# Strided and local attention followed by a spectral mix: PE's order written out with one mode between pieces, local heads with full rows, the last product made by groups of modes

## The chip, the cores and the metric

The kernel runs on one core of a Trainium2 chip. The metric is the time of one execution on the device, in microseconds, median of the runs. The engines are PE (matmul), DVE, ACT, POOL and SP; POOL and SP also issue the DMAs here. Inputs and output lie in HBM as float32; the kernel computes in float16 with float32 accumulation.

## What is computed

```python
# attention: q, k, v are (8, 8, 576, 64)
mask_local = (rel >= 0) & (rel < 32)                      # heads 0 to 3
mask_strided = (rel >= 0) & (pos_k % 32 == pos_q % 32)    # heads 4 to 7
attn = softmax(where(mask, q @ k.T / 8, -1e9)); x = attn @ v   # (8, 576, 512)
# spectral mix, w_r and w_i are (64, 512, 512)
X = rfft(x, axis=1)[:, :64]
Yr = einsum(Xr, w_r) - einsum(Xi, w_i); Yi = einsum(Xr, w_i) + einsum(Xi, w_r)
u = x + irfft(Yr + 1j * Yi, n=576)
out = u + relu(u @ w_ch)
```

`rel` is the query's position less the key's; the einsums multiply each of 64 modes with its own 512x512 matrix.

## The kernel before

The work goes in four stages.

**Strided heads** (loop L622 to L638). For each of 8 batches `load_str` (L176) fetches q, k, v; `str_front` turns q and k on PE into `qT` and `kz`; `str_scores` multiplies six blocks, with the mask added by a matmul with the identity, and ACT takes the exponential into one of two buffers `P`; `str_values` multiplies with v; `normalise` writes `xb`. `dft` (L428) is the forward Fourier transform as a matmul. `w_fetch` (L155) meanwhile fills 12 weight buffers of 512 KB each (`pw`). All of w_r and w_i goes through them as 128 tiles: the 64 modes for input channels 256 to 511 first (slot 0), then for 0 to 255 (slot 1). POOL issues these DMAs, the q and k loads and part of v, in order in its queue; SP issues the rest of v and the output.

**Local heads with slot 0** (L651 to L656). For each batch the code is written as `attn_loc`, `dft`, and `modes(b, 0)` with eight modes. In `attn_loc` two heads share the array as 64-row halves (`pr`), keys of the 32 positions before a block are multiplied as 32-row tiles (L376, L409). A mode is 16 matmuls of 128x128 weights with 16 columns (L471), after which its buffer is free for the next `w_fetch`. Eight modes fill one PSUM tile `y`; ACT copies it to `Y0`.

**Prepare with slot 1** (L661 to L663). `prepare` turns `xb` into `xT`, and computes for 5 row tiles x @ w_ch into `v0` and x itself into `xo`. `modes(b, 1)` then adds its `y` to `Y0` and gives `YT` (L485).

**Finish** (L664). For each batch the transpose `yy` of YT (L562) and its product with w_ch, `zz` (L571), then for each row tile two accumulations in PSUM: v0 plus the inverse transform `cA` of zz (L586, L589), and xo plus that of yy (L593, L596). ACT takes relu of the first into `rl` (L600), DVE adds the second (L601), and SP sends it out.

The order on each engine is not that of the code: a scheduler places each instruction by a cost of its own among those that are ready, within the waits for data and buffers.

Of the kernel before, what the change touches and what calls it, by code (L numbers as in the profile page):

```python
# [15 lines left out]
B = 8  # L16
# [10 lines left out]
NWBUF = 12  # L27


def _host_consts():  # L30
# [16 lines left out]
    A = np.zeros((2 * NM, S))  # L47
    for mm in range(NM):
        e = np.zeros(S // 2 + 1, dtype=np.complex128)
        e[mm] = 1.0  # L50
        A[mm] = np.fft.irfft(e, n=S)
        e[mm] = 1j
        A[NM + mm] = np.fft.irfft(e, n=S)

# [12 lines left out]
    k = np.arange(128)[:, None]  # L67
    q = np.arange(128)[None, :]
    own = np.where((q - k >= 0) & (q - k < STRIDE), 0.0, NEG)
    mo = np.tile(own, (1, 4))  # L70
    mm_ = np.zeros((128, 384))
    mm_[:64, :128] = np.tile(own[:64, :64], (1, 2))
    kk = np.arange(32)[:, None]
    qq = np.arange(32)[None, :]
    mm_[96:, 128:] = np.tile(np.where(qq < kk, 0.0, NEG), (1, 8))
    f16 = [a.astype(np.float16) for a in (Fl, Fs, A, ms[0], ms[1], mo, mm_)]
# [4 lines left out]
def kernel(  # L81
# [15 lines left out]
    ps_tp = ctx.enter_context(tc.tile_pool(name="ps_tp", bufs=2, space=PSUM))  # L97
    ps_sc = ctx.enter_context(tc.tile_pool(name="ps_sc", bufs=2, space=PSUM))
    ps_av = ctx.enter_context(tc.tile_pool(name="ps_av", bufs=2, space=PSUM))
    ps_y = ctx.enter_context(tc.tile_pool(name="ps_y", bufs=2, space=PSUM))  # L100

    def psum_tp():
        return ps_tp.tile([128, 1024], F16, tag="tp", name="tp")

    def psum_sc():
        return ps_sc.tile([128, 512], FP, tag="sc", name="sc")

    def psum_av():
        return ps_av.tile([128, 512], FP, tag="av", name="av")

    def psum_y():
        return ps_y.tile([128, 512], FP, tag="y", name="y")

    hosts = _host_consts()
    names = ["cFl", "cFs", "cA", "cM6", "cM5", "cMo", "cMm", "cI"]
# [7 lines left out]
    w_cp = consts.tile([128, 4, DM], F16, name="w_cp")  # L123
# [8 lines left out]
    Y0 = big.tile([128, NM, 4, 16], F16, name="Y0")  # L132
    YT = big.tile([128, 4, B, 2, NM], F16, name="YT")
    xb = [px.tile([128, 11, 256], F16, tag="xb", name="xb") for _ in range(B)]

    wctx = ctx.enter_context(ExitStack())
    pw = wctx.enter_context(tc.tile_pool(name="pw", bufs=NWBUF))
# [6 lines left out]
    Ps = [pat.tile([128, 2816], F16, name=f"P{i}") for i in range(2)]  # L144
    v16 = [pat.tile([128, 12, 132], F16, name=f"v16_{i}") for i in range(3)]

    def clear(i):
        nc.vector.memset(kzs[i], 0.0)
        nc.vector.memset(Ps[i], 1.0)
# [3 lines left out]
    w_tiles, w_chs = [], []  # L153

    def w_fetch(n=1):  # L155
        for _ in range(n):
            i = len(w_tiles)
            if i == 2 * NM and not w_chs:
                w_ch = pw.tile([128, 4, DM], F16, tag="w", name="w_ch")
                nc.gpsimd.dma_start(  # L160
                    w_ch, moe_w_ch.rearrange("(c p) e -> p c e", p=128)
                )
                w_chs.append(w_ch)
            if i >= 2 * NM:
                return
            half, m = 1 - i // NM, i % NM
            wt = pw.tile([128, 4, DM], F16, tag="w", name="wt")
            for ri, src in enumerate([moe_w_r, moe_w_i]):
                nc.gpsimd.dma_start(  # L169
                    wt[ds(64 * ri, 64)],  # L170
                    src[m, ds(256 * half, 256), :].rearrange("(p c) e -> p c e", c=4),
                )
            w_tiles.append(wt)


    def load_str(b, early=None):  # L176
        qn = pin.tile([128, 2, 2048], F16, tag="qn", name="qn")
        for i, src in enumerate([q, k]):
            nc.gpsimd.dma_start(
                qn[0:72, i, :],  # L180
                src[b, 4:8].rearrange("h (c r) d -> (h c) (r d)", r=32),
            )
        vg = v16[b % 3]
        v32 = pin.tile([128, 8, 128], FP, tag="v32", bufs=2, name="v32")
        for j, (a, z) in enumerate(JG):
            n = (z - a) * NCB
            for h in range(4):
                src = v[b, 4 + h].rearrange("(c r2 rp) d -> c r2 (rp d)", r2=16, rp=2)
                if j == 0:
                    nc.gpsimd.dma_start(vg[0:n, h, 2:130], src[:, a:z, :])  # L190
                else:
                    nc.sync.dma_start(v32[0:n, 4 * j - 4 + h, :], src[:, a:z, :])
        return qn, v32

    def load_loc(b):
        qn = pin.tile([128, 2, 2048], F16, tag="qn", name="qn")
        for i, src in enumerate([q, k]):
            nc.gpsimd.dma_start(
                qn[:, i, 0:1152],
                src[b, 0:4].rearrange("h (cb i) d -> (h cb) (i d)", i=18),  # L200
            )
        v32 = pin.tile([128, 20, 64], FP, tag="v32", bufs=2, name="v32")
        for t in range(5):
            nc.sync.dma_start(
                v32[0 : SCS[t], ds(4 * t, 4), :],
                v[b, 0:4, ds(128 * t, SCS[t]), :].rearrange("h s d -> s h d"),
            )
        return qn, v32
# [19 lines left out]
    def str_front(b, qn, v32, part):  # L228
        qT, kz, vg = qTs[b % 2], kzs[b % 2], v16[b % 3]
        if part == 0:  # L230
            nc.gpsimd.tensor_copy(out=vg[0:90, 4:12, 2:130], in_=v32[0:90])
        tp = psum_tp()
# [40 lines left out]
    def str_scores(b, t):  # L273
        qT, kz, P = qTs[b % 2], kzs[b % 2], Ps[b % 2]
# [4 lines left out]
        scp = psum_sc()  # L279
        nc.tensor.matmul(scp[:, 0 : 4 * n], idn, mask, start=True, stop=False)  # L280
        for h in range(4):
# [8 lines left out]
            out=P[0:n, ds(POFF[t], 4 * n)],  # L290
# [5 lines left out]
    def str_values(b, t):  # L296
        P, vg = Ps[b % 2], v16[b % 3]
        j, rp = STR[t]
        n = (JG[j][1] - JG[j][0]) * NCB
        avp = psum_av()  # L300
        av = avp[:, 0:264].rearrange("p (h c) -> p h c", c=66)
        for h in range(4):
            nc.tensor.matmul(
                av[:, h, 0:65],
                P[0:n, ds(POFF[t] + n * h, 128)],
# [13 lines left out]
    def attn_loc(b, qn, v32):  # L319
        qT, P, vg = kzs[b % 2], Ps[b % 2], v16[b % 3]  # L320
        nc.gpsimd.tensor_copy(  # L321
            out=vg[:, 0:8, 2:130],
            in_=v32[:, 0:16, :].rearrange("p (g i) d -> p g (i d)", i=2),
        )
        nc.gpsimd.tensor_copy(
            out=vg[0:64, 8:10, 2:130],
            in_=v32[0:64, 16:20, :].rearrange("p (g i) d -> p g (i d)", i=2),
        )
        for vi in range(2):
            for g in range(2):  # L330
                tp = psum_tp()
                for i in range(9):
                    for hp in range(2):
                        nc.tensor.transpose(  # L334
                            tp[ds(64 * hp, 64), ds(64 * i, 64)],
                            qn[ds(64 * hp, 64), vi, ds(64 * (9 * g + i), 64)],
                            idn[ds(64 * hp, 64), ds(64 * hp, 64)],
                        )
                nc.vector.tensor_copy(  # L339
                    out=qT[:, vi, 0:1152].rearrange("p (h s i) -> p h s i", h=2, i=18)[  # L340
                        :, :, :, ds(9 * g, 9)
                    ],
                    in_=tp[:, 0:576].rearrange("p (i h s) -> p h s i", h=2, s=32),
                )
        for hp in range(2):
            pr = ds(64 * hp, 64)
            for hh in range(2):
                scp = psum_sc()
                nc.tensor.matmul(scp, idn, cs["cMo"], start=True, stop=False)  # L349
                for t in range(4):  # L350
                    nc.tensor.matmul(  # L351
                        scp[:, ds(128 * t, 128)],
                        qT[pr, 1, ds(576 * hh + 128 * t, 128)],
                        qT[pr, 0, ds(576 * hh + 128 * t, 128)],
                        start=False,
                        stop=(t == 3),
                    )
                nc.scalar.activation(  # L358
                    out=P[:, ds(512 * (2 * hp + hh), 512)],
                    in_=scp,  # L360
                    func=ACTF.Exp,
                    scale=SCALE,
                )
            scp = psum_sc()
            nc.tensor.matmul(scp[:, 0:384], idn, cs["cMm"], start=True, stop=True)
            for hh in range(2):
                nc.tensor.matmul(
                    scp[0:64, ds(64 * hh, 64)],
                    qT[pr, 1, ds(576 * hh + 512, 64)],
                    qT[pr, 0, ds(576 * hh + 512, 64)],  # L370
                    start=False,
                    stop=True,
                    skip_group_check=True,
                )
                for t in range(1, 5):
                    nc.tensor.matmul(  # L376
                        scp[96:128, ds(128 + 128 * hh + 32 * (t - 1), 32)],
                        qT[pr, 1, ds(576 * hh + 128 * t - 32, 32)],
# [317 lines left out]
```

## Time and profile before

| | |
|---|---|
| median of 3 runs | 519.66 us (518.39 to 520.14) |
| profiled execution | 520.25 us, span 518.5 us |
| busy: PE, PEld, DVE, ACT, POOL | 388.7, 252.5, 205.7, 134.7, 190.5 us |
| chain that ended last: PE, DMA, DVE | 49%, 38%, 5% |
| DMA moved | 97.50 MB at 188 GB/s; HBM read 165.78 MB, written 9.44 MB |

Busy time is an average over stages with different limits, so the rows to read are those by stage, and within a stage what was waited for last. PE's busy time is not PE at its peak. A wait of an engine matters only where the engine is on the chain.

### The profile page before, as it was taken

To read this page: it belongs to the slowest core of one execution; us is meant where nothing else is said; L and a number is where in the kernel's file an instruction comes from. 1 tells how busy PE (TensorE), PEld (TensorE's weight loads), DVE (VectorE), ACT (ScalarE), POOL (GpSimd) and SP (SyncE) were. 2 spreads that over 40 slices of the span, in tenths; PEclk is the share of its full clock that TensorE was granted. 3 is DMA by queue.
4 is the path that set the end of the run, shared out by engine and by line. 5 is a ranking of instruction groups with operands and counts; after the bars stand their busy time and mean duration, and the time that the engine had idled before them with its cause. 6 is when DMAs were issued, how large, how long until landed. Compare 5 with 4: busy or idle time off the path is not lost.

```text
span 518.5 us, 11415 instructions
## 1 busy us (share of the span) xinstructions
PE 388.7 (75%) x4832; PEld 252.5 (49%) x4832; DVE 205.7 (40%) x426; ACT 134.7 (26%) x257; POOL 190.5 (37%) x353
## 2 busy tenths in 40 slices
PE   3867787699999972569989998798972222239996
PEld 2655555556666652247646655465562222224332
DVE  6545445632414302024113556766450110125564
ACT  2545446222122120101321222232210000005553
POOL 5655654325343143515344434432253444300000
PEclk9978657755556555555555689998785555559999
DMA  8999989999999759999998999999799999965454
GB/s 165 184 193 181 188 156 186 197 183 196 211 212 211 143 88 207 212 209 169 213 211 157 211 212 212 212 213 190 126 168 212 212 211 212 211 114 183 183 184 182
DMA packets 61634, 97.50 MB, mean 188 GB/s; under 512 B 31760, under 2 KB 39312, under 8 KB 61584
## 3 DMA queue, kind: packets, MB, share of 16 engines
q0 software_dynamic: 32080, 78.51, 80.3%
q1 hardware_dynamic: 28928, 17.73, 12.8%
q8 instruction: 38, 0.62, 0.4%
q10 hardware_dynamic: 576, 0.53, 0.3%
q14 instruction: 12, 0.10, 0.0%
HBM read 165.78 MB, written 9.44 MB: 338 GB/s over the span
## 4 chain that ended last, share of the span: by engine, by line
PE 49%; DMA 38%; DVE 5%; issue 2%; ACT 2%; POOL 2%; SPq 1%; POOLq 0%; ACTq 0%; DVEq 0%
DMA wt<-in_moe_w_i_dram 25%; PE y L471 6%; DMA qn<-in_k_dram 5%; PE y L439 4%; PE sc L538 4%; PE av L401 4%; DMA qn<-in_q_dram 4%; PE av L409 3%; PE tp L334 3%; PE sc L351 3%; PE sc L349 2%; PE sc L586 2%; DMA wt<-in_moe_w_r_dram 2%; PE av L596 2%; PE av L593 2%
## 5 line engine op out<-in xcount | busy, mean ns | idle before, releaser
L169 POOL DMA_DIRECT2D wt<-in_moe_w_r_dram x128 | 67.1, 524 | 149.4 <-PE y L471 64.6
L471 PE MATMUL y<-X,wt 128*128 128x16 f16 x2048 | 72.4, 192 | 56.8 <-DMA wt<-in_moe_w_i_dram 56.1
L471 PEld LDWEIGHTS <-wt 128*128 128x128 f16 x2048 | 67.1, 105 | 66.8 <-issue 64.9
L169 POOL DMA_DIRECT2D wt<-in_moe_w_i_dram x128 | 67.6, 528 | 54.6 <-DMA wt<-in_moe_w_i_dram 45.2
L538 PE MATMUL sc<-w_cp,xT 128*128 128x512 f16 (+1 forms) x160 | 55.3, 420 | 2.6 <-DVE xT L526 2.0
L216 DVE RECIPROCAL rec<-av 90x4 f32<-90x4 f32 (+2 forms) x80 | 14.5, 182 | 102.4 <-PE av L409 79.1
L485 DVE TENSOR_TENSOR YT<-y,Y 128x512 f16<-128x512 f32 x8 | 19.5, 2437 | 70.3 <-PE y L471 70.3
L546 ACT ACTIVATE v<-sc 128x512 f16<-128x512 f32 (+1 forms) x40 | 23.8, 595 | 65.9 <-PE sc L538 65.9
L547 DVE COPY xo<-tp 128x512 f16<-128x512 f16 (+1 forms) x40 | 27.7, 695 | 31.7 <-PE tp L545 31.6
L339 DVE COPY kz<-tp 128x576 f16<-128x576 f16 x32 | 23.8, 756 | 34.4 <-PE tp L334 33.9
L401 PE MATMUL av<-v,P 128*128 128x65 f16 (+1 forms) x160 | 32.1, 236 | 6.9 <-POOL v L321 5.3
L545 PE MATMUL tp<-cI_s,xT 128*128 128x128 f16 (+1 forms) x160 | 35.6, 234 | 1.5 <-DVE xo L547 1.5
L334 PE MATMUL tp<-cI_s,qn 64*64 64x64 f16 x576 | 23.4, 239 | 17.6 <-DMA qn<-in_q_dram 16.4
L217 DVE TENSOR_TENSOR xb<-av,rec 90x256 f16<-90x256 f32 (+2 forms) x80 | 34.9, 443 | 1.5
L601 DVE TENSOR_TENSOR osb<-av,rl 128x512 f32<-128x512 f32 (+1 forms) x40 | 26.9, 688 | 18.7 <-ACT rl L600 14.7
L358 ACT ACTIVATE P<-sc 128x512 f16<-128x512 f32 x32 | 18.3, 596 | 60.1 <-PE sc L351 60.0
L459 ACT ACTIVATE X<-y 64x256 f16<-64x256 f32 x32 | 12.1, 378 | 77.0 <-DVE X L457 76.7
L334 PEld LDWEIGHTS <-qn 64*64 64x64 f16 x576 | 18.5, 147 | 24.0 <-DMA qn<-in_q_dram 17.1
L409 PE MATMUL av<-v,P 32*32 32x65 f16 x128 | 29.4, 231 | 0.0
L579 ACT ACTIVATE zz<-y 128x512 f16<-128x512 f32 x8 | 4.8, 598 | 93.8 <-PE y L571 93.8
L538 PEld LDWEIGHTS <-xT 128*128 128x128 f16 (+1 forms) x160 | 16.9, 107 | 21.8 <-issue 6.0
L289 ACT ACTIVATE P<-sc 90x360 f16<-90x360 f32 (+1 forms) x48 | 23.0, 487 | 17.3 <-PE sc L282 15.5
(74 smaller groups left out, 624.7 us busy)
## 6 DMA issues: line engine op xcount, KB each, us to landing
wt<-in_moe_w_r_dram POOLq DMA_DIRECT2D x128, 256.0 KB, 9.4
wt<-in_moe_w_i_dram POOLq DMA_DIRECT2D x128, 256.0 KB, 9.6
out_dram<-osb SPq DMA_DIRECT2D x16, 512.0 KB
qn<-in_q_dram POOLq DMA_DIRECT2D x16, 288.0 KB, 7.5
qn<-in_k_dram POOLq DMA_DIRECT2D x16, 288.0 KB, 8.9
v<-in_v_dram SPq DMA_DIRECT2D x32, 128.0 KB
v<-in_v_dram SPq DMA_DIRECT2D x64, 45.0 KB
out_dram<-osb SPq DMA_DIRECT2D x8, 128.0 KB
```

The lines of the kernel that those rows point to most:

```text
L169: nc.gpsimd.dma_start(wt[ds(64 * ri, 64)], src[m, ds(256 * half, 256), :].rearrange("(p c) e -> p c e", c=4),)
L217: nc.vector.tensor_tensor(out=dst, in0=val.rearrange("p h (q c) -> p h c q", c=4), in1=rec[0:n, 0:pieces] .to_broadcast((n, pieces, 64)) . ...
L334: nc.tensor.transpose(tp[ds(64 * hp, 64), ds(64 * i, 64)], qn[ds(64 * hp, 64), vi, ds(64 * (9 * g + i), 64)], idn[ds(64 * hp, 64), ds(64 * ...
L339: nc.vector.tensor_copy(out=qT[:, vi, 0:1152].rearrange("p (h s i) -> p h s i", h=2, i=18)[:, :, :, ds(9 * g, 9)], in_=tp[:, 0:576].rearra ...
L401: nc.tensor.matmul(av[:, t, 0:65], lhs, vg[0 : SCS[t], 2 * t + h // 2, v_cols(h % 2)], start=True, stop=True,)
L409: nc.tensor.matmul(av[0:32, t, 0:65], P[96:128, ds(pm + 128 + 128 * hh + 32 * (t - 1), 32)], vg[96:128, 2 * (t - 1) + h // 2, v_cols(h % 2 ...
L471: nc.tensor.matmul(yv[:, mi, e, :], wt[:, c, ds(128 * e, 128)], Xh[half][:, c, :, :, m], start=(c == 0), stop=(c == 3),)
L538: nc.tensor.matmul(vp[0:n, :], xT[:, ch, cols], w_cp[:, ch, :], start=(ch == 0), stop=(ch == 3),)
L545: nc.tensor.transpose(tp[0:n, ds(128 * ch, 128)], xT[:, ch, cols], idn)
L546: nc.scalar.activation(out=v0[0:n, t, :], in_=vp[0:n, :], func=ACTF.Copy)
L547: nc.vector.tensor_copy(out=xo[0:n, t, :].rearrange("p (h q c) -> p h q c", h=2, c=4), in_=tp[0:n, 0:512].rearrange("p (h c q) -> p h q c" ...
L601: nc.vector.tensor_tensor(out=osb[0:n, i, :], in0=up[0:n, :], in1=rl[0:n, :], op=AluOp.add)
```

## The change

It does six things.

1. `tc.manual_schedule()`: each engine gets its instructions in the order in which the code issues them. The order is then written out by hand. In the local stage the loads come two or three batches ahead, the front of batch b + 1 is laid between the pieces of batch b, and one mode (`mode`, 16 matmuls, then `w_fetch`) stands after each two pieces. In slot 1 one mode stands between single turns and row tiles of `premix`, the former `prepare`.
2. Local heads without row tiling: keys are stored in `kz` with zeros in the other head's 64 rows, so that scores and values go with 128 rows. Scores of a block and of the 32 queries after it are one 160-column matmul, and the 32-row tiles are gone. `PS` and `PL` take the place of the two `P`.
3. YT is ordered by groups of 16 modes. For the first three groups `spec` makes transpose and product with w_ch (4 batches at a time) during slot 1; for the last one `spec_last` does so after the last mode. `cA`'s rows follow that order.
4. In the output, units of 128 rows; the last 64 rows of two batches share a unit. For odd row tiles xo is added by POOL to rl (two SBUF inputs) instead of by a PE matmul; the row addition of unit i comes two units behind its relu (`LAG`).
5. 13 weight buffers instead of 12; `w_cp` lies in one of them for a time, and `rl` takes slots there too. Weights are issued at t = 2 and t = 4 of a batch.
6. PSUM tiles are divided anew for each stage (`psum_pools`).

On PE in the local stage before (wt is a weight tile, y its output, qn the loaded q and k, kz the turned ones, sc scores, av values; numbers are buffers, later ones higher), from one mode to a run of eleven:

```order
L334 MATMUL tp_3058<-cI_s_83,qn_2275 64x64
L471 MATMUL y_2487<-X1_86,wt_1886 128x16
...
L401 MATMUL av_2825<-v16_0_112,P1_111 128x65
L349 MATMUL sc_3105<-cMo_s_81,cI_s_83 128x512
L471 MATMUL y_2487<-X1_86,wt_1905 128x16
L351 MATMUL sc_3105<-kz0_108 128x128
L439 MATMUL y_2838<-cFl_s_76,xb_92 128x192
...
L471 MATMUL y_2487<-X1_86,wt_2157 128x16
L471 MATMUL y_2487<-X1_86,wt_2176 128x16
L471 MATMUL y_2853<-X1_86,wt_2561 128x16
L334 MATMUL tp_3384<-cI_s_83,qn_2641 64x64
```

Between wt_1886 and wt_1905 stand the values of two heads, the transposes of nearly two front pieces and the masks of two score tiles; from wt_2157 to wt_2561 eleven modes follow each other. The same place in the program after the change:

```order
L391 MATMUL sc_2356<-cMa_s_71,cI_s_73 128x480
L407 MATMUL sc_2356<-qT0_95,kz0_97 128x160
L360 MATMUL tp_2364<-cI_s_73,qn_1643 64x64
L497 MATMUL y_2384<-X1_75,wt_1820 128x16
L407 MATMUL sc_2404<-qT0_95,kz0_97 128x160
L407 MATMUL sc_2410<-qT0_95,kz0_97 128x64
L497 MATMUL y_2384<-X1_75,wt_1852 128x16
L360 MATMUL tp_2436<-cI_s_73,qn_1643 64x64
L428 MATMUL av_2457<-v16_2_103,PL_100 128x65
L436 MATMUL av_2457<-v16_2_103,PL_100 128x65
L497 MATMUL y_2384<-X1_75,wt_1904 128x16
```

Now a mode stands after each one or two pieces, and no two modes are neighbours. On DVE at the end of the program before (xo and xT belong to `prepare`, YT_88 is the sum of both slots, osb an output tile):

```order
L547 COPY xo_6244<-tp_6294 64x512
L485 TENSOR_TENSOR YT_88<-y_5060,Y0_87 128x8x64
L485 TENSOR_TENSOR YT_88<-y_6305,Y0_87 128x8x64
L568 COPY yy_6440<-tp_6435 128x512
L568 COPY yy_6505<-tp_6500 128x512
L601 TENSOR_TENSOR osb_6449<-av_6453,rl_6456 128x512
```

All of prepare lies ahead of the last six YT adds, and every yy behind the last of them. After the change, from the last but one YT add to the first output:

```order
L511 TENSOR_TENSOR YT_77<-y_6003,Y0_76 128x4x16x8
L591 COPY xo_6258<-tp_6289 128x512
L610 COPY yy4_4384<-tp_6300 32x512
L591 COPY xoh3_4371<-tp_6391 64x512
L511 TENSOR_TENSOR YT_77<-y_6271,Y0_76 128x4x16x8
L610 COPY yy0_4380<-z_6480 32x512
L610 COPY yy1_4381<-z_6480 32x512
L784 TENSOR_TENSOR osb_6512<-u_6509,rl_6495 128x512
```

The premix copies have moved between the YT adds, and of yy only the last group's 32 rows of a batch are behind the last add, a batch at a time. The core of the diff:

```diff
-NWBUF = 12
+NWBUF = 13
...
+    ctx.enter_context(tc.manual_schedule())
...
+    Y0 = big.tile([128, 4, 4, 16, 16], F16, name="Y0")
+    YT = big.tile([128, 4, 4, 16, 16], F16, name="YT")
...
+            for t in range(3):
+                todo.append((160 * t, 576 * (h % 2) + 128 * t, 160))
+        for i, (col, s0, n) in enumerate(todo):
+            nc.tensor.matmul(
+                scp[:, ds(col, n)],
+                kzs[par][:, hp, ds(s0, 128)],
+                qTs[par][:, ds(s0, n)],
...
+    def spec_mm(g, bq, tp, zp):
         for e in range(4):
...
+            lhs = YT[:, e, g, ds(8 * bq, 8), :].rearrange("p x m -> p (x m)")
+            nc.tensor.transpose(tp[:, ds(128 * e, 128)], lhs, idn)
+        for e in range(4):
+            lhs = YT[:, e, g, ds(8 * bq, 8), :].rearrange("p x m -> p (x m)")
             nc.tensor.matmul(
...
+                zp, lhs, w_chs["n"][:, e, :], start=(e == 0), stop=(e == 3)
+            )
+
+    def spec_out(g, b, tp, zp):
+        src, dst = ds(32 * (b % 4), 32), ds(32 * g, 32)
+        nc.scalar.activation(out=zzs[b][dst], in_=zp[src, :], func=ACTF.Copy)
+        nc.vector.tensor_copy(out=yys[b][dst], in_=tp[src, 0:512])
...
+            if t == 2:
+                load_v16(b + 2)
+                w_fetch()
+            if t == 4 and len(w_tiles) < NWBUF - B + 1 + b:
+                w_fetch()
...
+        work = [
+            scores[0], front[0], scores[1], ends[0], front[1], values[0], scores[2],
+            values[1], scores[3], ends[1], front[2], values[2], front[3], values[3],
+            lambda: dft(b, 0),
+        ]
...
+        for mi in range(8):
+            upto = -(-len(work) * (mi + 1) // 8)
+            for w in work[n:upto]:
+                w()
+            n = upto
+            mode(0, 8 * b + mi)
...
+    for m in range(NM):
+        mode(1, m)
+        upto = min(len(work), -(-len(work) * (m + 1) // 60))
+        for w in work[n:upto]:
+            w()
+        n = upto
+        if m >= 16 and m % 16 in (4, 8):
+            spec(m // 16 - 1, 0 if m % 16 == 4 else 1)
...
+        nc.scalar.activation(out=rl, in_=vp, func=ACTF.Relu)
+        if t % 2:
+            nc.gpsimd.tensor_tensor(out=rl, in0=rl, in1=xos[b][:, t, :], op=AluOp.add)
...
+    LAG = 2
+    for i in range(len(units) + LAG):
+        if i < len(units):
+            b, t = units[i]
+            unit_v(i)
+            if t == 1 and b + 1 < B:
+                if b + 1 == 4:
+                    spec_last(1)
+                spec_out(3, b + 1, *held[(b + 1) // 4])
+        if i >= LAG:
+            unit_u(i - LAG)
```

More of the change, by code (lines that the diff above doesn't have):

```diff
@@ L185, in load_str @@
[L185 to L208, printed above, removed]
+                v16[b % 3][0 : (z - a) * NCB, h, 2:130], str_v(b, h, a, z)
+            )
@@ L367, in attn_loc, with loc_values @@
+    def loc_values(b, h):
+        vg = v16[b % 3]
+        av = psum("av")[:, 0:330].rearrange("p (t c) -> p t c", c=66)
+        for t in range(5):
+            off = 1024 * h + (256 * t if t < 4 else 960)
+            nc.tensor.matmul(
+                av[:, t, 0:65],
+                PL[:, ds(off, 128)],
+                vg[:, 2 * t + h // 2, v_cols(h % 2)],
+                start=True,
+                stop=(t == 0),
+            )
+            if t > 0:
                 nc.tensor.matmul(
-                    scp[0:64, ds(64 * hh, 64)],
@@ L493, in prepare @@
-    def prepare(b):
-        xT = ptr.tile([128, 4, S], F16, tag="xT", bufs=2, name="xT")
-        for ch in range(2):
-            tp = psum_tp()
+        wt = w_tiles[slot * NM + m]
+        for e in range(4):
+            for c in range(4):
+                nc.tensor.matmul(
+                    yv[:, mi, e, :],
+                    wt[:, c, ds(128 * e, 128)],
+                    Xh[half][:, c, :, :, m],
+                    start=(c == 0),
+                    stop=(c == 3),
+                )
@@ new lines, in rows_u @@
+    def rows_u(b, t, up, add):
+        cols = out_cols(t)
+        if add:
+            xo = xos[b][:, t, :] if t < 4 else xoh[b // 2]
+            nc.tensor.matmul(up, idn, xo, start=True, stop=(t == 4))
+        if t < 4:
+            nc.tensor.matmul(up, cs["cA"][:, cols], yys[b], start=not add, stop=True)
+            return
+        for i in range(2):
+            nc.tensor.matmul(
+                up[ds(64 * i, 64), :],
+                cs["cA"][:, cols],
+                yys[b - 1 + i],
+                start=not add,
+                stop=True,
+                skip_group_check=True,
+            )
@@ new lines, with spec_last @@
+    n = 0
+    for m in range(NM):
[6 more added lines that the diff above has]
+            spec(m // 16 - 1, 0 if m % 16 == 4 else 1)
+    psum_pools(z=2, v=3, u=3)
+    units = []
+    for b in range(B):
+        units += [(b, t) for t in range(4)]
+        if b % 2:
+            units.append((b, 4))
+    held, rls, osbs = {}, {}, {}
+    def spec_last(bq):
+        held[bq] = psum("z", half=True), psum("z")
+        spec_mm(3, bq, *held[bq])
```

652 lines of the change are left out of this document (344 added, 308 removed).

## The prediction, before the run

> **What bounds the kernel now.** I read the slices of the page first, then busy time by stage, then the timeline where the DMA share falls, and last the chain of waits from the last weight on. In the slices each digit is a fortieth of the span, about 13 us:
>
> ```profile
> PEclk9978657755556555555555689998785555559999
> DMA  8999989999999759999998999999799999965454
> GB/s 165 184 193 181 188 156 186 197 183 196 211 212 211 143 88 207 212 209 169 213 211 157 211 212 212 212 213 190 126 168 212 212 211 212 211 114 183 183 184 182
> ```
>
> Up to slice 35 the DMA is full nearly everywhere, with 212 GB/s as its ceiling, and it falls in slices 13, 14, 18, 21, 27 and 28. From slice 36 on it runs at half. So there are two stages with two limits: the loads up to about 460 us, and the output after that. Busy time by stage (columns: PE, PEld, DVE, ACT, POOL, granted clock, DMA share, GB/s):
>
> ```profile
> 104.00:160.00 56.00, 55.42 (x745) 36.12 (x746) 18.82 (x42) 12.49 (x24) 22.71 (x42) 0.50 1.02 201
> 160.00:200.00 40.00, 31.36 (x452) 20.81 (x449) 7.28 (x16) 9.23 (x18) 11.63 (x23) 0.54 0.79 147
> 200.00:273.00 73.00, 57.31 (x735) 37.36 (x735) 17.46 (x38) 12.49 (x24) 29.93 (x56) 0.50 1.04 204
> 273.00:286.00 13.00, 12.18 (x180) 8.76 (x179) 4.52 (x13) 1.35 (x3) 5.66 (x11) 0.50 0.84 158
> 286.00:351.00 65.00, 59.33 (x729) 38.20 (x728) 39.86 (x79) 17.92 (x31) 25.41 (x50) 0.92 1.06 212
> 351.00:390.00 39.00, 31.78 (x468) 20.86 (x467) 21.37 (x32) 7.14 (x12) 13.71 (x28) 0.81 0.90 162
> 468.00:511.00 43.00, 43.00 (x192) 17.02 (x191) 25.57 (x41) 24.10 (x44) 0.00 (x0) 1.00 0.53 193
> ```
>
> A full DMA shows as a share of 1.06. What is missing to 1.06, times the length, is DMA time lost: 104 to 160 us 2.1, 160 to 200 us 10.2, 200 to 273 us 1.4, 273 to 286 us 2.7, 351 to 390 us 5.9. Together **22.3 us**. The timeline shows what the largest hole is made of:
>
> ```profile
> 170.72 0.65 PE L471 MATMUL y<-X,wt 128*128 128x16 f16 x16
> 171.67 0.51 POOL L169 DMA_DIRECT2D wt<-in_moe_w_r_dram  x1 [6.98 <-PE y L471]
> 176.19 0.68 PE L471 MATMUL y<-X,wt 128*128 128x16 f16 x16
> 177.17 0.51 POOL L169 DMA_DIRECT2D wt<-in_moe_w_r_dram  x1 [4.47 <-PE y L471]
> 184.16 0.51 POOL L169 DMA_DIRECT2D wt<-in_moe_w_r_dram  x1 [5.96 <-PE y L471]
> 186.01 3.93 PE L471 MATMUL y<-X,wt 128*128 128x16 f16 x129
> 201.95 1.17 PE L334 MATMUL tp<-cI_s,qn 64*64 64x64 f16 x36 [9.84 <-DMA qn<-in_q_dram]
> ```
>
> All weight buffers were full, PE did attention of two batches and only one mode (16 matmuls) every 5 to 7 us; POOL could issue a weight only when a mode had freed its buffer. Then eight modes came at once, and PE in its turn waited for data. What a weight costs the DMA is seen where it alone sets the pace:
>
> ```profile
> 405.37 0.64 PE L471 MATMUL y<-X,wt 128*128 128x16 f16 x16 [1.87 <-DMA wt<-in_moe_w_i_dram]
> 407.83 0.64 PE L471 MATMUL y<-X,wt 128*128 128x16 f16 x16 [1.81 <-DMA wt<-in_moe_w_i_dram]
> ```
>
> One weight each 2.46 us; 128 of them are 315 us that no order can shorten. After the last weight the chain reads:
>
> ```profile
> 460.40 0.65 PE y L471 x16
> 461.14 2.45 DVE YT L485
> 463.64 0.93 PE tp L562 x7
> 464.57 1.71 PE y L571 x4
> 473.08 0.21 PE sc L589
> 476.12 0.33 PE av L593
> 477.11 0.86 PE y L571 x4
> 483.39 0.86 PE y L571 x4
> 514.59 0.68 DVE osb L601
> ```
>
> From 460.40 to the end at 518.5 are **58.1 us**, and PE is the chain: 6.28 us a batch (483.39 - 477.11), a 512-wide matmul at the full clock 0.22, a 64-row one 0.33, and at half clock 0.43 (1.71 / 4).
>
> **The change part by part.**
>
> *Local stage and second half (20 us off).* One mode now stands between small pieces of attention, and later of premix, so a buffer comes free about once in 2.5 us and POOL always has a weight to issue. This holds if PE needs less than the DMA for each batch. The DMA needs 8 x 2.46 = 19.7 us for weights and some more for q, k and v. For PE, the rows of one batch before:
>
> ```profile
> 112.28 0.24 PE L401 MATMUL av<-v,P 128*128 128x65 f16 x1
> 112.45 0.23 PE L409 MATMUL av<-v,P 32*32 32x65 f16 x1
> 112.61 0.23 PE L401 MATMUL av<-v,P 128*128 128x65 f16 x1
> 104.82 1.03 PE L351 MATMUL sc<-kz 64*128 64x128 f16 x8
> ```
>
> Alternating full and 32-row tiles starts one matmul each 0.165 us. The 16 pairs of a batch take 5.3 us; as full tiles at half clock, 65 columns in 0.055 us (65 of the 512 that take 0.43), 36 of them take 2.0. PE thus needs 3.3 us less a batch, on top of being spread. Score matmuls keep their column sum: 4 x (480 + 480) + 2 x (512 + 448) = 5760 against 5632 before, so nothing there. [...]
>
> In the second half (64 modes, 158 us of DMA) PE's work at half clock is 160 x 0.43 = 69 us of premix, 336 transposes of 0.13 (0.93 / 7) = 44, 64 modes of 0.65 = 42, and six new Z groups of 4 x (0.43 + 0.13) = 13: 168 us at worst, and much less at the 0.81 to 0.92 that the prepare stretches were granted. I keep about 2 of the 22.3 us as lost in waits of the written order and take 20.
>
> *Strided stage (0, between -5 and +5).* PE, ACT and DVE do the same pieces; one P buffer instead of two, three score buffers instead of two. SP's v loads and POOL's q, k loads are issued a batch earlier, one more weight (buffer 13) is fetched, and POOL issues weights after v16 instead of before the batch. The cost at the start:
>
> ```profile
> L149 DVE MEMSET P<- 128x2816 f16 x2 | 4.8, 2405 | 1.1 <-issue 1.1
> ```
>
> 0.85 ns an element. The new memsets (three v16 of 1584, PS 2342, PL as 2080 words) are 6.1 + 1.8 us instead of 4.8, so the first copy of qT comes about 3 us later. The DMA loads under it, which is why I cost it at 0; uncovered it is 3.
>
> *Tail (14 us off).* Only the last group of 16 modes is left when the last weight has come. Rows for the pieces (DVE, ACT, POOL):
>
> ```profile
> L485 DVE TENSOR_TENSOR YT<-y,Y 128x512 f16<-128x512 f32 x8 | 19.5, 2437 | 70.3 <-PE y L471 70.3
> L601 DVE TENSOR_TENSOR osb<-av,rl 128x512 f32<-128x512 f32 x32 | 21.5, 689 | 15.9 <-ACT rl L600 14.7 <-PE av L596 1.1
> L600 ACT ACTIVATE rl<-sc 128x512 f32<-128x512 f32 x32 | 17.7, 596 | 6.5 <-PE sc L589 6.5
> L568 DVE COPY yy<-tp 128x512 f16<-128x512 f16 x8 | 3.3, 411 | 3.3 <-PE tp L562 3.3
> L321 POOL CAST v<-v 128x1024 f16<-128x1024 f32 x8 | 8.4, 1045 | 19.6 <-DMA v<-in_v_dram 19.6
> ```
>
> Head: mode 0.65, YT add between 0.69 (same elements, L601) and 2.44 (L485, whose scattered output goes away): I take 0.7; four transposes and four matmuls at half clock 2.2; zz 0.6; waits 0.35: 4.5 us. Rows: 112 matmuls (8 per batch for v, 6 for u) x 0.217 = 24.3, the four shared 64-row units 4 x (2 x 0.22 + 4 x 0.33) = 7.0, second Z 1.2: 32.5, or 4.1 a batch instead of 6.28; 1 for the clock's rise and 2 for waits between engines. End: the last add 0.68 and 3.2 from there to the span's end as before. Sum 4.5 + 32.5 + 3 + 3.9 = 44, against 58.1: 14 off. Beside PE's 32.5, ACT has 36 x 0.6 + 8 x 0.6 = 26, DVE 36 x 0.69 + 8 x 0.41 = 28, and the output at twice the DMA share of 0.53 could go 364 GB/s where 9.44 MB in 34 us ask 278, so PE stays last.
>
> POOL adds half of the xo terms, 16 adds of 512, a two-input operation that the trace doesn't show: at least 0.52 us (half of the 1024-wide cast), at most the 1.05 of a whole one taken twice, 2.1. Two units need 7 matmuls, 1.5 us, so below 1.5 it is hidden; the nearest row, one operand each from two casts of 512, gives 1.05, which I take. At 2.1 the tail is 16 x 0.6 = 10 us longer. [...]
>
> **Sum.** 520.25 (the profiled execution, span 518.5 and 1.75 around it; the median of the runs is 519.66) - 20 - 14 = **486 us**.
>
> **The rivals.**
> 1. *The holes stay in another form.* Now PE stands in line: a piece that waits for its exp or its q, k holds the mode behind it, and with it POOL's next weight. For it: PE waited 9.84 us for q above. Against: q and k are now asked for two batches ahead, and PE needs less than the DMA. With 15 of the 20 us still lost: 501.
> 2. *The tail is held by POOL or by the output buffers* (adds at 2.1 us, as above): 10 us back, 496.
> 3. *The clock stays at half, slower.* Pieces set between waits for weights could keep PE at the 0.50 of 104 to 286 us. Decided by the clock in the tail: at half its 32.5 us become 65, and the second half's 168 us pass the DMA's 158 by 10: 486 + 32.5 + 10 = 528. Against: those same 512-wide matmuls were granted 1.00 from 468 us on. [...]
> 4. *Nothing moves:* stalls of the written order equal both gains, 517 to 523.
>
> **How the numbers follow.** Forecast 0.64 (478 to 494), rival 1 0.15, rival 2 0.12, rival 3 0.05, rival 4 0.04 (half of it within 0.3%, which is what a measurement of this kernel can tell from no change, half above). The range goes from 520.25 - 27 (all holes and the 5 of the strided stage) - 18 (no waits, a clock at once) = 475 up to 505, which takes in rivals 1 and 2. Faster 0.91, same 0.02, slower 0.07.
>
> **What would show it.** The DMA share at 1.04 or more from the first mode to the last weight, and the last mode's start near 440 us; PE waiting for weights, not POOL for PE; a YT add below 1 us; 4.1 us a batch in the tail at clock 1.00; the last add some 40 us behind the last mode. Wrong if the DMA share still falls below 0.9 in a slice, if a Pool add is above 1.5 us, or if the tail's clock is 0.5.

## The result, and the profile after

The changed kernel takes **481.43 us** (median of 4 runs, 480.62 to 486.65), against 519.9 us for the kernel before in the same session: a ratio of 0.929 with a 95% interval of [0.922, 0.936]. It was forecast at 486, between 475 and 505. The profiled execution took 480.62 us, the shortest of the four, with a span of 478.8.

The slices of the page:

```profile
PEclk9986678859895565555565659677887796795998
DMA  8989999989999999999999999999999999992685
GB/s 164 198 171 185 189 179 187 196 164 213 211 215 212 209 210 210 211 213 211 198 187 206 213 213 213 209 213 213 210 212 212 212 212 212 212 212 47 255 321 216
```

The holes that before had in slices 13, 14, 18, 21, 27 and 28 (counted from 0) are gone. From slice 9 on, what is left of them is a dent in slices 19 and 20, and the end is shorter and denser: 321 GB/s in a slice, where the end of the kernel before never passed 184. Busy time by stage (columns as before: PE, PEld, DVE, ACT, POOL, granted clock, DMA share, GB/s):

```profile
104.00:160.00 56.00, 40.82 (x862) 32.31 (x861) 19.64 (x43) 19.86 (x36) 24.47 (x45) 0.77 1.06 207
160.00:200.00 40.00, 27.23 (x457) 20.63 (x457) 10.91 (x25) 8.95 (x16) 18.25 (x35) 0.54 1.08 210
200.00:273.00 73.00, 44.16 (x728) 33.24 (x725) 16.12 (x37) 16.86 (x31) 31.95 (x60) 0.55 1.05 205
273.00:286.00 13.00, 8.16 (x118) 5.66 (x117) 3.98 (x10) 1.68 (x4) 5.31 (x11) 0.50 1.06 212
351.00:390.00 39.00, 31.08 (x406) 20.60 (x405) 18.52 (x37) 11.19 (x19) 16.04 (x31) 0.81 1.06 212
```

In the first row PE starts 862 matmuls in 40.82 us of busy time, where before needed 55.42 for 745, and the granted clock is 0.77 instead of 0.50. The DMA share is 1.05 to 1.08 in these rows, where a full DMA shows as 1.06. POOL hardly waits for PE's modes any more (us in total, number of waits, longest; before, then after):

```profile
POOL wt L169 <- PE y L471: 64.6, 23, 7.2
POOL wt L159 <- PE y L497: 6.0, 7, 1.2
```

The dent is one wait in POOL's line, in the timeline:

```profile
228.46 0.51 POOL L159 DMA_DIRECT2D wt<-in_moe_w_i_dram  x1 [0.55 <-DMA wt<-in_moe_w_i_dram]
237.00 1.04 POOL L349 CAST v<-v 128x1024 f16<-128x1024 f32 x1 [8.03 <-issue]
238.75 0.40 POOL L353 CAST v<-v 64x256 f16<-64x256 f32 x1 [0.71 <-DMA v<-in_v_dram]
239.26 0.51 POOL L159 DMA_DIRECT2D wt<-in_moe_w_r_dram  x1
```

POOL stood at the casts of v and issued no weight for 10 us. The profile names no releaser for the first of them; that its v was still loading is the likely reading, since the second waited for just that. From the last mode on, the chain of waits (start, length, what):

```profile
435.50 0.65 PE y L497 x16
436.25 0.70 DVE YT L511
437.00 0.61 PE z L600 x4
437.60 1.72 PE z L603 x4
439.35 0.59 ACT zz L609
439.98 0.59 PE v L618
440.57 0.43 PE v L616
...
454.59 0.34 PE v L621 x2
...
461.95 0.34 PE v L621 x2
...
469.31 0.36 PE v L621 x2
469.69 0.61 ACT rl L773
```

The last mode starts at 435.50 (before: 460.40), and from there to the end of the span are 43.3 us (before: 58.1). So **24.9 us came from the load stage and 14.8 from the tail**, where 20 and 14 were forecast (one profiled run of each kernel). Two groups and the last adds on VectorE:

```profile
L511 DVE TENSOR_TENSOR YT<-y,Y 128x512 f16<-128x512 f32 x8 | 5.5, 692 | 14.2 <-PE y L497 14.2
L775 POOL TENSOR_TENSOR rl<-rl,xo 128x512 f32<-128x512 f32 x16 | 18.5, 1159 | 25.9 <-ACT rl L773 25.9
```

```profile
470.28 1.89 DVE L784 TENSOR_TENSOR osb<-u,rl 128x512 f32<-128x512 f32 x3 [0.31 <-ACT rl L773]
```

The last add ends at 472.17, and 6.7 us of the span are left. The DMA share in 40 slices of 472.17 to 478.84 us shows that output moves in the first 2.7 of them only:

```profile
DMA  0699999995998892000000000000000000000002
```

In the last 4.0 us nothing moves but one packet of 8 KB on an instruction queue. In the kernel before, the last 1.3 us were empty.

### The profile page after: what moved, and what is told of

The parts are those of the page before. It is cut to its first block, busy times and chain, and to the rows that moved or that the text cites. A ratio compares the mean times of both kernels' runs of the same rounds, so it can differ in the third digit from the quotient of the medians.

```text
span 478.8 us, 11198 instructions
## 1 busy us (share of the span) xinstructions
PE 333.7 (70%) x4680; PEld 233.4 (49%) x4680; DVE 204.8 (43%) x443; ACT 158.6 (33%) x293; POOL 210.5 (44%) x369
## 4 chain that ended last, share of the span: by engine, by line
DMA 59%; SPq 24%; PE 11%; issue 3%; POOL 2%; DVE 0%; ACT 0%; DVEq 0%; POOLq 0%
DMA v<-in_v_dram 24%; SPq L225 23%; DMA wt<-in_moe_w_i_dram 22%; DMA wt<-in_moe_w_r_dram 12%; PE v L616 2%; PE sc L581 2%; PE v L618 2%; SPq L219 1%; PE u L636 1%; DMA cFl_s<-cFl 1%; PE y L497 1%; POOL wt L159 1%; PE u L634 1%; PE z L603 1%; PE tp L589 0%
## 5 line engine op out<-in xcount | busy, mean ns | idle before, releaser
L590 ACT ACTIVATE v<-sc 128x512 f16<-128x512 f32 x32 | 18.9, 597 | 93.8 <-PE sc L581 93.8
L421 ACT ACTIVATE PL<-sc 128x480 f16<-128x480 f32 (+1 forms) x48 | 27.4, 578 | 58.7 <-PE sc L407 58.6
L591 DVE COPY xo<-tp 128x512 f16<-128x512 f16 x32 | 22.1, 691 | 48.6 <-PE tp L589 48.4
L428 PE MATMUL av<-v,PL 128*128 128x65 f16 x160 | 18.2, 218 | 26.6 <-POOL v L349 15.7
L327 PE MATMUL av<-v,PS 90*128 90x65 f16 (+1 forms) x192 | 18.7, 220 | 17.4 <-ACT PS L313 10.4
L775 POOL TENSOR_TENSOR rl<-rl,xo 128x512 f32<-128x512 f32 x16 | 18.5, 1159 | 25.9 <-ACT rl L773 25.9
L784 DVE TENSOR_TENSOR osb<-u,rl 128x512 f32<-128x512 f32 x36 | 24.1, 689 | 6.9 <-ACT rl L773 4.7
L313 ACT ACTIVATE PS<-sc 90x360 f16<-90x360 f32 (+1 forms) x48 | 23.2, 488 | 8.6 <-PE sc L306 7.3
L407 PE MATMUL sc<-qT,kz 128*128 128x160 f16 (+1 forms) x160 | 25.8, 296 | 0.0
L306 PE MATMUL sc<-qT,kz 128*128 128x90 f16 (+1 forms) x192 | 22.6, 249 | 4.6 <-DVE kz L290 4.6
L462 PEld LDWEIGHTS <-xb 108*128 108x128 f16 (+2 forms) x176 | 20.0, 128 | 9.2 <-issue 5.7
```

What stands on the lines that cost most here:

```text
L306: nc.tensor.matmul(scp[:, ds(n * h, n)], kz[:, rp, ds(288 * h + a * NCB, 128)], qT[:, ds(288 * h + a * NCB, n)], start=False, stop=(h == 3),)
L313: nc.scalar.activation(out=PS[0:n, ds(POFF[t], 4 * n)], in_=scp[0:n, 0 : 4 * n], func=ACTF.Exp, scale=SCALE,)
L407: nc.tensor.matmul(scp[:, ds(col, n)], kzs[par][:, hp, ds(s0, 128)], qTs[par][:, ds(s0, n)], start=False, stop=(i == len(todo) - 1),)
L421: nc.scalar.activation(out=dst, in_=src, func=ACTF.Exp, scale=SCALE)
L462: nc.tensor.matmul(xp[:, ds(192 * cp, 192)], xb[b][0:n, base + t, ds(128 * cp, 128)], F[0:n, t, :], start=(i == 0), stop=(i == len(tiles) ...
L591: nc.vector.tensor_copy(out=xo[pr].rearrange("p (h q c) -> p h q c", h=2, c=4), in_=tp[pr, 0:512].rearrange("p (h c q) -> p h q c", h=2, c=4),
```

## The experiments

Each run was compared with the kernel before on the same chip (519.79 to 522.38 us in those sessions). Two questions stood open: which part of the change closed the holes, and what sets the tail. On the first there were three theories: **A**, the scheduler lets attention run batches ahead of the modes, and any written order cures that; **B**, only a mode between small pieces keeps the DMA full; **C**, full rows relieve PE, and that closes the holes.

### 1. Before, with its own order written out

```diff
+    ctx.enter_context(tc.manual_schedule())
```

> The kernel before, with one line more: every engine takes its instructions in the order of the code (attention of a batch, its transform, its eight modes; then prepare and eight modes), nothing interleaved by hand, 12 buffers, row tiles kept, tail unchanged. Theory A (the holes come from attention that the scheduler let run batches ahead of the modes): the last mode starts at 435 to 445 us instead of 460.4, the tail keeps its 58 us, so 495 to 505 us. Theory B (only a mode between small pieces keeps the DMA full): PE stands at each wait inside attention and inside prepare, the holes stay or grow, 515 us or more.

525.97 us, a ratio of 1.011 [1.008, 1.014]: 1% slower. Busy time by stage:

```profile
104.00:160.00 56.00, 46.97 (x613) 29.38 (x612) 13.56 (x30) 12.32 (x23) 17.43 (x33) 0.50 0.80 153
273.00:286.00 13.00, 11.42 (x174) 8.20 (x173) 3.59 (x10) 0.76 (x2) 3.93 (x8) 0.50 0.75 142
```

The holes moved to where PE stands inside a batch; the last mode starts at 462.19. A falls in this form: a written order is not enough by itself. Theory B had 515 us or more for it.

### 2. Before, with full rows for the local heads

The scheduler, the order of the code and the old tail stay; scores, values and masks of the local heads are those of the change. With them come one `P` for the strided heads and a part of the k copies on ScalarE; there are 12 buffers.

```diff
-                        tile_position=(96, 0),
...
+                    PL[:, ds(1024 * h + 256 * t - 128, 128)],
+                    vg[:, 2 * (t - 1) + h // 2, v_cols(h % 2)],
```

> The kernel before with the scheduler, in which only the local heads are taken from the change (full rows, zero halves in kz, one P for the strided heads). Theory A: PE has 3 us less work in a batch but the scheduler still puts attention ahead, some of the 22.3 us of lost DMA time comes back, at most 10: 508 to 518 us. Theory C (the saved PE time is what closes the holes): the last mode starts near 440 us, 498 to 503 us.

**495.4 us**, a ratio of 0.952 [0.949, 0.956], and the last mode starts at 434.95, as early as in the changed kernel.

```profile
104.00:160.00 56.00, 50.62 (x1003) 39.75 (x999) 24.61 (x58) 27.69 (x51) 23.12 (x43) 0.87 1.06 207
160.00:200.00 40.00, 8.56 (x206) 7.47 (x207) 2.83 (x4) 2.51 (x4) 16.14 (x32) 0.53 1.07 212
```

Full rows alone give the whole gain of the load stage. With the scheduler still running attention ahead (1003 matmuls in the first row, little in the second), the modes lag less: POOL waits 20.6 us for them instead of 64.6. Neither the thirteenth buffer nor the earlier loads are needed for this.

### 3. The changed kernel, with row tiles back

```diff
-                kzs[par][:, hp, ds(s0, 128)],
-                qTs[par][:, ds(s0, n)],
...
+                    qT[pr, 1, ds(576 * hh + 128 * t, 128)],
+                    qT[pr, 0, ds(576 * hh + 128 * t, 128)],
```

> The changed kernel with the local heads in row tiles as before, at the same places between the modes. Theory A: PE needs about 3 us more a batch and has 8 to spare, the DMA stays full: 480 to 485 us. Theory C: the DMA share falls in the local stage and the time goes up by 3 us a batch or more, 495 us and above.

485.32 us, a ratio of 0.935 [0.929, 0.942]; the last mode starts at 438.30.

```profile
104.00:160.00 56.00, 55.49 (x767) 36.67 (x767) 18.14 (x39) 10.92 (x21) 25.20 (x47) 0.50 1.05 203
160.00:200.00 40.00, 39.53 (x543) 25.80 (x545) 11.96 (x26) 9.23 (x18) 17.03 (x33) 0.50 1.09 211
```

The order written by hand closes the holes without full rows, too; the thirteenth buffer and the earlier loads, which this kernel keeps, may have a part in that. But PE is then busy for 95 of 96 us at clock 0.50: it just keeps up. C's number (495 or more) falls, though its point, that PE is at its limit with row tiles, is what the rows show.

What row tiles cost is in PE's busy time with the values (`av`) and with the scores and their masks (`sc`) alone. In this kernel, `av` and then `sc` (columns: PE busy and number of matmuls, granted clock, DMA share, GB/s):

```profile
104.00:160.00 56.00, 17.28 (x108) 0.50 1.05 203
104.00:160.00 56.00, 17.44 (x105) 0.50 1.05 203
```

and in the changed kernel, in a stage with nearly the same clock:

```profile
200.00:273.00 73.00, 8.25 (x108) 0.55 1.05 205
200.00:273.00 73.00, 16.58 (x78) 0.55 1.05 205
```

A batch has 36 value matmuls either way. They take 5.8 us in row tiles (17.28 / 3) and 2.75 with full rows (8.25 / 3), 0.160 and 0.076 us each; the prediction had 0.165 and, as an estimate, 0.055. The score matmuls of a batch, masks among them, are 42 in row tiles and 26 with full rows, and take 7.0 and 5.5 us (17.44 / 105 x 42 and 16.58 / 3). So the value matmuls in alternation take twice as long each as with full rows, at clocks of 0.50 and 0.55; what the time goes to was not measured.

### 4. Pieces of a batch in a block, then its eight modes

```diff
         for mi in range(8):
-            upto = -(-len(work) * (mi + 1) // 8)
-            for w in work[n:upto]:
-                w()
-            n = upto
```

All pieces now run ahead of this loop.

> The changed kernel, in which the local stage does all pieces of a batch first and then its eight modes one behind the other. Theory A: thirteen buffers are 32 us of DMA, a batch of pieces is some 12 us, so POOL never lacks a free buffer: within 3 us of the changed kernel, 480 to 485. Theory B: the DMA share falls once a batch, 8 times 1 to 3 us, 490 to 505.

482.2 us, a ratio of 0.926 [0.923, 0.930], and a DMA share of 1.05 or more in each of the stages from 104 to 390 us. B falls. POOL waited for modes 15 times, 4.8 us at most: with thirteen buffers a block of pieces is bridged. Whether twelve would do was not tried.

### 5. The two halves of "full rows"

Both on the kernel before: full rows for the scores alone (a), for the values alone (b).

```diff
+                    PL[96:128, ds(1024 * h + 256 * t - 128, 32)],
...
+                    tile_position=(96, 0),
```

(a: values from row tiles)

```diff
+                    out=PV[:, 2 * hp + hh, :, 0:128],
+                    in_=scp.rearrange("p (t x) -> p t x", t=4),
```

(b: scores of row tiles, spread into the padded buffer)

> The kernel before (its scheduler, its tail) with full rows for the scores of the local heads alone; their values keep the alternation of full and 32-row tiles. Both halves together had given 495.4 us, the last mode at 435.4 and a clock of 0.87 in 104 to 160 us. Theory V (the alternation in the values is what overloads PE, 0.165 us a matmul instead of 0.055): the load stage keeps its holes, DMA share below 0.95 somewhere in 160 to 290 us, last mode 452 or later, 512 to 521. Theory S (the small tiles of the scores keep the granted clock at 0.50, and the clock is what PE lacks): clock above 0.65 in 104 to 160 us, last mode before 448, 497 to 508.

> The kernel before with full rows for the values of the local heads alone; their scores stay in row tiles (the exp of the small tiles goes out in three instructions a pair of heads instead of one, 4 more a batch on ScalarE). Theory V: PE is relieved of some 3 to 4 us a batch, the holes close, last mode 435 to 442, 494 to 503, whatever the clock. Theory S: the clock stays at 0.50 to 0.55 in 104 to 160 us and the holes close in part only, last mode 445 to 455, 504 to 514.

(a) 503.16 us, a ratio of 0.964 [0.961, 0.967], last mode at 445.46; (b) 500.62 us, 0.956 [0.953, 0.960], last mode at 441.05. The first row of the windows, of (a) and of (b):

```profile
104.00:160.00 56.00, 54.49 (x779) 39.45 (x775) 20.73 (x45) 21.75 (x39) 23.02 (x43) 0.65 1.06 206
```

```profile
104.00:160.00 56.00, 55.05 (x867) 38.10 (x861) 21.32 (x46) 16.41 (x45) 22.44 (x42) 0.56 1.06 205
```

Before lost 22.3 us in holes, 2.8 a batch if they are spread over the eight, and either half takes most of that away: 19.3 us by (b), 14.9 by (a), 25.5 together, measured on the last mode (460.40 - 441.05, 445.46 and 434.95). At (a) S's forecast holds and V's fails (512 or more); at (b) V's holds and S's fails (504 or more): neither theory has both halves.

The values gain though the clock is only 0.56. The scores gain although their column sum is nearly the same, and the clock of 0.65 isn't all of it. PE's time with `sc` at nearly the same clock, in row tiles (b) and with full rows (a):

```profile
104.00:160.00 56.00, 25.36 (x156) 0.56 1.06 205
200.00:273.00 73.00, 14.16 (x70) 0.57 1.00 197
```

That is 6.8 us for the 42 matmuls of a batch against 5.3 for the 26. In 104 to 160 us the granted clock is 0.50 with both halves in row tiles, 0.65 or 0.56 with one, and 0.87 with neither.

### 6. Which order is needed at all?

The changed kernel under the scheduler (a), and experiment 2 in the written order of the old code (b).

```diff
-    ctx.enter_context(tc.manual_schedule())
```

```diff
+    ctx.enter_context(tc.manual_schedule())
```

> The changed kernel with its instructions ordered by the scheduler again instead of in written order; the full rows, the tail by groups of modes and all else stay. Theory F (PE's overload in the local stage was the cause, full rows cure it, the order is not needed): the last mode starts between 435 and 441 us, the time is 480 to 488. Rival W (written order is needed once modes and pieces stand in one program): the scheduler lets attention run ahead again, PE's full rows notwithstanding, the last mode is later than 445 and the time is above 490.

> The kernel before with full rows for the local heads, and written order in addition (its code order: nine pieces of a batch, then its modes, nothing interleaved by hand); the tail is the old one. Written order alone had cost 5.5 us, full rows alone had gained 24.7. Theory F: with full rows PE has slack and the waits inside a batch are absorbed by 13 buffers, so the last mode starts near 436 to 444 and the time is 495 to 503. Rival W (code order leaves PE at waits for exp and values whatever it costs per batch): last mode above 450, 510 or more.

(a) **483.55 us**, 0.931 [0.924, 0.938], last mode at 437.74, tail 43.0 us. F's forecast holds: the written order is worth nothing that these intervals can tell. (b) 509.15 us, 0.979 [0.971, 0.987], last mode at 446.38, between the two forecasts: the old code order loses 11 us in the load stage even with full rows. (This kernel has 12 buffers, not the 13 of the expectation.) POOL's longest wait there:

```profile
118.25 0.52 POOL L169 DMA_DIRECT2D wt<-in_moe_w_r_dram  x1 [17.07 <-PE y L474]
```

For 17 us no mode freed a buffer. Experiment 4 has the modes in a block as well, but its pieces overlap within the batch, its q and k come two batches ahead, and it has 13 buffers; which of these does it was not separated.

### 7. The early groups of Z made after the last mode

```diff
-        if m >= 16 and m % 16 in (4, 8):
-            spec(m // 16 - 1, 0 if m % 16 == 4 else 1)
...
+    for g in range(3):
+        for bq in range(2):
```

> The changed kernel with the three early groups of Z (modes 0 to 47) made after the last mode instead of between the modes; the same instructions, only later. Six more group halves stand ahead of the tail's rows: PE 6 x (0.43 + 0.13) x 4 = 13 us at half clock, 7 at the full one, ACT 24 x 0.6 = 14 us of copies. If the early groups are what shortens the tail, 43.3 us become 51 to 57 and the time 489 to 495. Rival: the tail is set by the output's transfer, which would start later by the same amount, so nothing is hidden there either; but if the tail's order has slack, less than 4 us are lost, 482 to 485.

509.62 us, 0.979 [0.970, 0.988]: far above either number. From the chain of waits:

```profile
440.95 0.64 PE y L497 x16
...
446.20 1.88 PE z L603 x4
448.11 0.59 ACT zz L609
...
449.91 0.60 ACT zz L609
450.55 1.86 PE z L603 x4
...
469.81 0.58 PE v L618
```

The six halves do not overlap: each takes 4.1 to 4.4 us, four matmuls at a clock of 0.50 (1.7 to 1.9 us) and then four copies, before the next may use the buffer. The first row starts 28.9 us after the last mode instead of 4.5. I had added up engine times (14 us) where a chain (25 us) rules. The other 5.4 us of the longer span come ahead of it: the last mode starts at 440.95 instead of 435.50. In this arrangement, doing three quarters of Z under the weights is worth 24 us, more than the whole gain of 14.8 over the old tail; late groups that overlap were not tried, so how much of it any tail would need stays open.

### 8. No add on POOL

```diff
-        if t % 2:
-            nc.gpsimd.tensor_tensor(out=rl, in0=rl, in1=xos[b][:, t, :], op=AluOp.add)
...
-        rows_u(b, t, up, add=(t % 2 == 0))
+        rows_u(b, t, up, add=True)
```

> The changed kernel with all xo terms of the tail added by PE (an extra matmul each, as for the even units) instead of half of them by POOL. PE gets 16 more matmuls of 512 columns, 16 x 0.217 = 3.5 us. If PE sets the tail (my prediction's reading), 484 to 486 and 4.1 us a batch instead of 3.7; if the output or the engines that follow PE set it, 481 to 482.5 and 3.7 a batch.

479.84 us, 0.924 [0.917, 0.931]; not to be told from the changed kernel, and below both forecasts.

```profile
432.35 0.65 PE y L497 x16
...
453.36 0.34 PE v L621 x2
...
461.58 0.34 PE v L621 x2
```

```profile
470.77 1.89 DVE L782 TENSOR_TENSOR osb<-u,rl 128x512 f32<-128x512 f32 x3 [0.39 <-ACT rl L773]
```

Two batches of rows lie between the shared units of 453.36 and 461.58: 4.1 us each, against 3.7 in the changed kernel (454.59 to 461.95). From the last mode to the end of the last add are 40.3 us, against 36.7: 3.6 more, just the 16 x 0.217 = 3.5 us of PE. **PE sets the pace of the rows.** But only 3.9 us follow the last add (span 476.6), instead of 6.7. The output is not what differs. Here, too, it ends 2.7 us after the last add, as the slices of 472.66 to 476.60 us show:

```profile
DMA  0078999989999997589949699600000000000000
```

What is shorter is the empty stretch behind it: 1.3 us instead of 4.0. It is 1.3 us in all seven profiled kernels without adds on POOL in the tail, the kernel before among them, and 3.6 to 4.0 in the six with them. So these adds take 3.6 us off the rows and cost 2.7 at the end. What fills the stretch, the views of the profile don't name.

### 9. The casts of v on ScalarE

```diff
-            nc.gpsimd.tensor_copy(
...
+                nc.scalar.activation(
```

> The changed kernel with the casts of the local heads' v (two instructions a batch, 1.05 and 0.5 us or so) made by ScalarE between two score pieces instead of by POOL, in whose line they stand ahead of weight issues. In the changed kernel POOL stood 8.0 us at the cast of 237 us for v, and the DMA share fell to 0.91 in 234 to 247 us, 2 us lost. Theory: no weight is held by v any more, no share below 1.03 from 104 us on, last mode 432 to 434, 477 to 480. Rival: ScalarE now stands where POOL stood, the exp behind it and with it PE and the modes come late; no gain or 2 to 6 us lost, 481 to 488.

482.46 us, 0.923 [0.920, 0.926], last mode at 439.80: no gain. The wait moved, as the rival said:

```profile
PE av L435 <- ACT v L352: 59.5, 8, 18.4
```

PE waited 59.5 us in 8 waits for ScalarE's casts (15.7 us in 5 waits for POOL's before that edit), and POOL 53.7 us for PE's modes. ScalarE in its turn waited 40.1 us in 4 waits for loads of v: what is late is v itself. Asking for it earlier was not tried.

## Why the prediction was right, and where it was not

**Load stage (20 off; measured 24.9).** That buffers were freed too late by PE, and that the DMA would then be full, is shown: POOL's wait for modes fell from 64.6 to 6.0 us, and the share is 1.05 to 1.08. (The five losses of the prediction are divided by 1.06 as well; only so do they give 22.3.) What it had wrong is the weight of the parts. *"PE thus needs 3.3 us less a batch, on top of being spread"* made the order the cause and the rows a bonus. In fact the rows are enough without the order (last mode at 435), and the order as laid by hand is enough without the rows (438; 460 with neither); of the written order the scheduler gives up nothing measurable. The condition *"if PE needs less than the DMA for each batch"* is barely met with row tiles: experiment 3 has PE busy for 95 of 96 us. The 3.3 us were near for the values (5.8 - 2.75 = 3.1 a batch). What I left at nothing were the scores, 1.5 us a batch (7.0 - 5.5), and the rise of the clock (0.50 to 0.77 in 104 to 160 us). The 2 us kept as lost were not lost.

The gain of 24.9 is more than the holes' 22.3, and where the rest comes from stays open. The early part (0, between -5 and +5) can't be told: the first copy of qT came 3.5 us later (12.91 against 9.40; forecast 3), while the DMA moved 184 GB/s up to 104 us against 181. And kernels with nearly the same load stage differ: their last mode came at 432.35 (experiment 8), 435.50 and 440.95 us (experiment 7), with 6.4, 9.6 and 10.4 us as POOL's longest wait for a local v. That spread is as large as the miss.

**Scores with full rows.** The prediction priced them by their column sum and had *"nothing there"*. The time did not go by the column sum: the 5632 columns of a batch took 7.0 us in row tiles (experiment 3, clock 0.50), the 5760 with full rows 5.5 (the changed kernel, 0.55); in experiment 5, at 0.56 and 0.57, it was 6.8 and 5.3. Whether the rows of a tile or the number of matmuls (42 and 26) makes the difference was not separated.

**Tail (44 after the last mode; measured 43.3).** Two errors cancel, and that the sum is so near is luck. The head came out at 4.48 (439.98 - 435.50, forecast 4.5), the YT add at 0.69 and POOL's add at 1.16 (taken 0.7 and 1.05).

The rows took 29.7 us (439.98 to 469.67) instead of 32.5 + 3. The term "2 x 0.22 + 4 x 0.33" of the shared units took each 64-row matmul at 0.33, but they run in pairs:

```profile
454.21 0.38 PE L616 MATMUL v<-v0h,cI_s 128*128 128x512 f16 x1
454.52 0.41 PE L621 MATMUL v<-zz,cA_s 128*64 128x512 f16 x2
454.86 0.39 PE L634 MATMUL u<-xo,cI_s 128*128 128x512 f16 x1
```

The pair holds PE for 0.34 us, and the full matmul ahead of it for 0.31 instead of 0.22, so the four units are 4 x (2 x 0.31 + 2 x 0.34) = 5.2 and not 7.0. PE was busy without a gap (29.70 of 29.70 us from 440.00 on), so the 2 us of waits were not needed. The last six u matmuls, some 1.3 us, run beside the last Relu and are not in the 29.7. The 1 us for the clock's rise is a term that no run shows: here the first three row matmuls start 0.38 to 0.43 us apart and those from 441.45 us on 0.22, which makes some 0.6 us. The rest of the difference, under 1 us, is not placed.

The end was put at 3.9 from the start of the last add on and took 9.2 from the end of the rows: 0.6 for the last Relu, 1.9 for three adds instead of one, 2.7 of output, and 4.0 in which nothing moves. The 3.2 that I took over from the kernel before were 1.9 of output and 1.3 of that. Experiment 8 puts the difference of 2.7 us down to the adds on POOL, which the prediction had priced by their pace alone.

**The rivals.** Rival 1 (holes in another form) did not come true in the changed kernel, beyond the dent of 234 to 247 us; it is what happened to the written order in experiments 1 and 6b. Rival 2 fell with POOL's 1.16 us, though POOL's adds cost 2.7 us at the end; rival 3 fell, since 286 to 430 us were granted 0.79 to 0.81 and the tail 0.96 (440 to 454 us) and 1.00 (454 to 467). In experiment 7 the clock did stay at 0.50 from 441 to 469.8 us, where PE was busy for 17.2 of 28.8. Rival 4 fell with the ratio.

## What to carry to other kernels

When a transfer shows holes, look first at whether the engine that frees its buffers is at its limit in just that stage (here PE, 55.4 of 56 us at clock 0.50): here some 4 us a batch of relief closed nearly all of them, and a second edit added almost nothing. Small tiles that alternate with full ones cost more here than the zeros that a padded tile computes (5.8 us a batch for the values against 2.75). In a tail, price dependent steps as a chain and not as engine sums (25 us against 14 in experiment 7), and look at what follows the last byte of output too (4.0 us here, 1.3 in the kernel before).

## What was not expected of the hardware

- **The granted clock stayed at 0.50 with PE busy all the time.** In experiment 3 PE was busy for 55.49 of 56 us with row tiles and was granted 0.50; with full rows, 0.77 at 40.82 us (the changed kernel) and 0.87 at 50.62 (experiment 2). With one half in full rows (experiment 5) it was 0.65 at 54.49 us and 0.56 at 55.05. So in these rows the clock does not go by PE's busy time; what it goes by was not measured.
- Two matmuls on the two 64-column halves of the array start almost together (two of 0.40 us span 0.41), and yet nothing is gained: with the full matmul ahead of them they hold PE for 0.65 us, as three full ones do.
- With adds on POOL in the tail, the program ends 3.6 to 4.0 us after the last byte of output, without them 1.3.
- The chain counts 25.44 us (213.18 to 238.62) for a load of v beside the weights; SP was occupied with issuing ten of these loads from 186.45 to 238.58.
- The output reached 321 GB/s in a slice, while the loads of the changed kernel never passed 215.
